# Dealing hidden features in steps of four, with 8 KB rows of w_out, in a fused attention and MLP kernel

## The chip, the core and the metric

The kernel runs on one core of one Trainium2 chip. Its time is that of one execution on the device, in microseconds. A core has five engines with an instruction stream each: TensorE (PE in the profile, its weight loads PEld), VectorE (DVE), ScalarE (ACT), GpSimd (POOL) and SyncE (SP). Transfers run on 16 DMA engines. Matmuls write to eight accumulator banks of 128 partitions and 512 four-byte words (PSUM); all else lies in the on-chip buffer (SBUF).

## The reference

There are 4 batches, 8 heads, 768 tokens and 64 features a head. Linear attention with a decay `lam` per head is computed in blocks of tokens, and its result, as rows of 512 features, goes through an MLP of 2048 hidden features with a "snake" activation.

```
intra = (q_b @ k_b.T * Dmask) @ v_b                   # inside a block; Dmask[i,j] = lam**(i-j), i >= j
inter = (q_b * lam_pow) @ kv_state                    # from the blocks before
out_b = intra + inter
kv_state = lam_block * kv_state + (k_b * rev_pow).T @ v_b

x = out as (3072 tokens, 512 features)
h = x @ w_in                                          # 512 x 2048
s = sin(alpha * h)
g = h + s * s / (alpha + 1e-9)                        # alpha: one number for each of the 2048 features
y = g @ w_out                                         # 2048 x 512
```

The order of the 2048 hidden features is free, as long as w_in's columns, alpha and w_out's rows follow the same one.

## The kernel before

Tokens are worked in six steps t of 128 tokens for all four batches, so a step has 512 columns. The MLP of a step is its group g. The hidden features are 16 blocks f of 128. Weights stand in four tiles of 512 features each: `w_in0` to `w_in3` (128 partitions by 4 pieces of x's features by 512 columns) and `w_out0` to `w_out3` (128 partitions by 4 blocks by 512). Block f takes columns `(f % 4) * 128` onward of `w_in` tile `f // 4`, one after the other; partition p of `w_out` tile i has the four rows `i * 512 + f * 128 + p`, each 2 KB in memory. All these loads turn four-byte numbers into two-byte ones and are issued by GpSimd, each into the same queue (q0); a transfer can be issued when the eighth before it has landed.

The first step is written out by hand. Its keys come in their natural form and are turned by TensorE (`turn_k0`, L383, with weight loads that take every second element); masks and the first hidden blocks run in halves of 256 columns (`hidden_half`, L458), as soon as two of the batches are done. `w_in0` is loaded in two parts of 256 columns, so that blocks 0 and 1 need the first part and blocks 2 and 3 the second. Between these matmuls stand `spin` matmuls on a constant tile. `alpha` is loaded as 16 rows of 128 and turned by one transpose (L204).

All that follows is the string `ORDER`: one word for each piece of work, in the order in which it is given to the engines. Each engine takes its own pieces strictly in that order, so a piece that waits holds up all behind it on its engine.

| word | piece | engine |
|---|---|---|
| `I`i, `W`i | load w_in tile i, w_out tile i | GpSimd queue |
| `r`t, `R`t, `n`t, `v`t | load raw keys, raw queries (four transfers each), natural keys, values (two each) of step t | GpSimd queue |
| `d`t.p | decay half the natural keys (L263) | GpSimd |
| `k`t.p, `j`t.p | turn half the keys, half the queries (L242) | VectorE |
| `F`t.p:banks | scores of two batches, into four banks (L252) | TensorE |
| `m`t.p.a | mask of bank a (L258) | VectorE |
| `K`t, `S`t.n, `B`/`C` | new state: products (L272), sum (L281, in step 0 a copy on ScalarE), cast on ScalarE or GpSimd | TensorE, VectorE |
| `O`t:banks | outputs: `carried` (64 matmuls) and `inside` (32), into four banks (L293, L302) | TensorE |
| `x`t.a | bank a of the outputs to x (L312) | VectorE |
| `h`g.f:bank | hidden block f, four matmuls (L324) | TensorE |
| `s`g.f | sine (L329) | ScalarE |
| `q`, `P`, `Q` g.f | square, on ScalarE, or on VectorE in two ways | ScalarE, VectorE |
| `t`g.f | finish: g = h + s²/alpha (L344); it frees the bank of h | VectorE |
| `u`g.m.part:bank | 128 rows of the result, with four hidden blocks (L351), needs `w_out` tile `part` | TensorE |
| `o`g.m | copy and store | ScalarE, SyncE |

Raw tiles have one buffer each, so the loads of step t+1 wait until step t's have been turned. `inside` runs over pairs of batches:

```
for a in range(NA):            # for pair 0, and then again for pair 1
    for u in range(2):
        for n in range(NQ):
            ... O[a][half[n], 2 * pr + u] += v.T @ masked scores
```

so that every one of the four banks gets its last matmul in the second pass.

Of the kernel before, what the change touches and what calls it, by code (L numbers as in the profile page):

```python
# [10 lines left out]
FP32 = mybir.dt.float32  # L11
# [5 lines left out]
s0.0 s0.1 P0.0 P0.1 I1 h0.7:6 s0.2 h0.5:5 s0.3 t0.0 q0.2 t0.1 h0.4:4 h0.6:2 I2 h0.9:7 t0.2 q0.3 t0.3 s0.4 s0.5  # L17
h0.8:0 P0.4 P0.5 s0.6 q0.6 t0.6 s0.7 s0.8 t0.4 q0.7 h0.11:1 s0.9 t0.5 h0.10:3 s0.10 P0.8 t0.8 q0.9 q0.10 t0.9
s0.11 d0.1 I3 h0.12:2 s0.12 W0 t0.7 u0.1.0:5 r1 h0.15:4 t0.10 q0.11 k1.0 q0.12 h0.13:7 s0.13 t0.12 W1 h0.14:6
t0.11 s0.14 s0.15 R1 u0.0.0:0 u0.3.0:3 q0.13 W2 k1.1 q0.14 u0.1.1 q0.15 t0.14 d0.0 K0:21 S0.1 u0.3.1 t0.13 W3  # L20
t0.15 j1.0 u0.2.0:1 S0.0 u0.2.1 j1.1 F1.0:4672 m1.0.0 m1.0.2 m1.0.3 u0.2.2 u0.3.2 u0.1.2 m1.0.1 F1.1:7246 m1.1.2
v1 u0.3.3 u0.1.3 o0.3 o0.1 m1.1.3 C0.1 u0.0.1 m1.1.1 C0.0 m1.1.0 O1:3745 x1.0 x1.2 x1.3 R2 u0.0.2 u0.2.3 o0.2
u0.0.3 x1.1 o0.0 r2 j2.0 h1.0:7 s1.0 k2.0 Q1.0 h1.1:0 h1.2:2 h1.3:4 s1.1 q1.1 t1.0 t1.1 F2.0:6351 m2.0.0 n1 n2
m2.0.1 s1.2 s1.3 k2.1 q1.2 t1.2 q1.3 h1.4:7 s1.4 h1.5:0 s1.5 q1.4 q1.5 h1.6:3 t1.3 s1.6 m2.0.2 h1.7:6 m2.0.3
t1.4 s1.7 h1.8:2 t1.5 q1.6 q1.7 h1.10:4 t1.6 s1.8 h1.9:5 s1.9 s1.10 t1.7 j2.1 h1.12:7 u1.0.0:1 q1.8 t1.8 q1.9
t1.9 q1.10 t1.10 h1.11:3 d1.1 d1.0 s1.11 K1:06 u1.0.1 h1.13:2 q1.11 t1.11 h1.14:5 u1.2.0:3 v2 S1.0 d2.1 S1.1
d2.0 K2:40 u1.2.1 s1.12 q1.12 s1.13 q1.13 h1.15:6 t1.12 t1.13 S2.0 u1.0.2 s1.14 r3 q1.14 t1.14 R3 s1.15
F2.1:4572 q1.15 S2.1 t1.15 u1.2.2 m2.1.0 B2.0 u1.1.0:0 v3 B1.0 m2.1.2 m2.1.1 B1.1 u1.0.3 u1.2.3 o1.2 B2.1 m2.1.3
O2:5672 j3.0 u1.1.1 u1.1.2 k3.0 x2.0 x2.1 o1.0 x2.3 x2.2 F3.0:4156 m3.0.0 u1.1.3 o1.1 h2.0:7 s2.0 m3.0.1 h2.1:2
k3.1 q2.0 s2.1 q2.1 j3.1 m3.0.2 h2.2:0 s2.2 n3 d3.0 u1.3.0:1 h2.3:4 u1.3.1 q2.2 t2.0 t2.1 t2.2 s2.3 d3.1  # L30
F3.1:3257 m3.1.1 m3.1.2 m3.0.3 u1.3.2 q2.3 K3:02 S3.1 h2.4:5 S3.0 m3.1.3 m3.1.0 R4 s2.4 q2.4 h2.5:6 h2.6:2 s2.5
s2.6 q2.5 t2.3 t2.5 u1.3.3 q2.6 t2.6 j4.0 r4 h2.7:0 s2.7 o1.3 h2.10:4 q2.7 t2.7 h2.8:7 s2.8 v4 O3:2613 t2.4
h2.9:0 x3.0 x3.2 h2.13:5 q2.8 s2.9 x3.3 s2.10 n4 d4.1 h2.11:2 x3.1 u2.0.0:1 q2.9 h2.12:6 t2.8 t2.9 u2.0.1 q2.10
t2.10 h3.0:3 s2.11 q2.11 t2.11 k4.0 s2.12 q2.12 t2.12 u2.0.2 s2.13 q2.13 F4.0:4207 m4.0.0 m4.0.2 t2.13 m4.0.1
B3.0 h2.14:6 s2.14 u2.3.0:4 q2.14 h2.15:0 s2.15 q2.15 u2.3.1 t2.14 k4.1 h3.2:5 m4.0.3 s3.0 q3.0 t2.15 t3.0
h3.1:6 s3.1 q3.1 s3.2 h3.3:2 r5 t3.1 u2.0.3 u2.1.0:7 q3.2 t3.2 s3.3 j4.1 h3.4:0 q3.3 t3.3 u2.1.1 d4.0 u2.3.2
o2.0 s3.4 q3.4 t3.4 u2.1.2 F4.1:6315 m4.1.3 B3.1 u2.3.3 o2.3 m4.1.1 u2.1.3 o2.1 m4.1.0 m4.1.2 u2.2.0:2 K4:04
S4.1 S4.0 O4:1365 h3.5:4 s3.5 h3.6:0 x4.0 u3.1.0:7 x4.1 h3.8:1 s3.6 x4.2 q3.5 t3.5 q3.6 k5.0 h3.7:6 v5 u2.2.1
x4.3 t3.6 s3.7 q3.7 s3.8 u3.0.0:3 u2.2.2 q3.8 h3.9:5 s3.9 q3.9 h3.10:4 s3.10 q3.10 t3.7 R5 j5.1 j5.0 t3.8 u3.0.1
h3.11:0 u2.2.3 t3.9 t3.10 s3.11 q3.11 t3.11 o2.2 u3.1.1 h3.12:1 F5.0:6042 h3.13:5 m5.0.0 u3.1.2 m5.0.3 m5.0.1  # L40
# [16 lines left out]
def kernel(  # L57
# [11 lines left out]
    nc = tc.nc  # L69
    P = nc.NUM_PARTITIONS  # L70

    B, H, S, D = q.shape
    T = 128
    NT = S // T
    NA = 4
    NQ = H // NA
    R = T // 32
    DM, DFF = moe_w_in.shape
    NDC = DM // P
    NFC = DFF // P  # L80
# [5 lines left out]
    consts = ctx.enter_context(tc.tile_pool(name="consts", bufs=1))  # L86
# [11 lines left out]
    def bank(nm, n):  # L98
        return psum.tile([P, 512], FP32, name=nm, tag=f"b{n}")

    V, G, A = nc.vector, nc.gpsimd, nc.scalar
# [5 lines left out]
    half = [slice(D * n, D * n + D) for n in range(NQ)]  # L107
# [4 lines left out]
    raw, nat = {}, {}  # L112
# [20 lines left out]
    w_in_sb = [wpool.tile([P, NDC, 512], BF16, name=f"w_in{i}") for i in range(4)]  # L133
    w_out_sb = [wpool.tile([P, 4, DM], BF16, name=f"w_out{i}") for i in range(4)]

    def load_w_in(i, parts=1, only=None):
        w = 512 // parts
        for j in range(parts) if only is None else [only]:
            for n in range(NQ):
                G.dma_start(out=w_in_sb[i][half[n], :, j * w:(j + 1) * w], in_=moe_w_in[  # L140
                    n * 256:(n + 1) * 256, i * 512 + j * w:i * 512 + (j + 1) * w].rearrange("(c p) g -> p c g", p=D))

    def load_w_out(i):
        G.dma_start(out=w_out_sb[i][:], in_=moe_w_out[i * 512:(i + 1) * 512, :].rearrange("(f p) d -> p f d", p=P))
# [5 lines left out]
    alpha_fp = consts.tile([NFC, P], FP32, name="alpha_fp")  # L150
    A.dma_start(out=alpha_fp[:], in_=moe_alpha.rearrange("(f p) -> f p", p=P))
# [17 lines left out]
    idf = consts.tile([NFC, NFC], FP32, name="idf")  # L169
    V.tensor_scalar(out=iden[:], in0=dist[:], scalar1=0.0, scalar2=None, op0=ALU.is_equal)  # L170
    V.tensor_copy(out=idf[:], in_=iden[0:NFC, 0:NFC])
# [31 lines left out]
    a_ps = bank("a_ps", 5)  # L203
    nc.tensor.transpose(out=a_ps[:, 0:NFC], in_=alpha_fp[:], identity=idf[:])  # L204
# [92 lines left out]
    def inside(t, pr):  # L297
        for a in range(NA):
            for u in range(2):
                for n in range(NQ):  # L300
                    b = 2 * pr + u
                    nc.tensor.matmul(out=att["O"][a][half[n], b, :], lhsT=nat["v", t][:, b, 4 * n + a, :],  # L302
                                     rhs=st[t, pr][:, a, u, n, :], start=False, stop=True,
                                     skip_group_check=True)

    def outputs(t, bks):
        carried(t, bks)
        inside(t, 0)
        inside(t, 1)
# [11 lines left out]
    def hidden(g, f, n):  # L321
        hps[g, f] = bank("hps", n)
        for c in range(NDC):
            nc.tensor.matmul(out=hps[g, f][:], lhsT=w_in_sb[f // 4][:, c, (f % 4) * P:(f % 4 + 1) * P],  # L324
                             rhs=xt[g][:, c, :], start=(c == 0), stop=(c == NDC - 1))
# [94 lines left out]
    A.copy(out=alpha_sb[:], in_=a_ps[:, 0:NFC])  # L420
    cut(0)
    cut(1)
    load_w_in(0, 2, 0)
    cut(2)
    cut(3)
    load_w_in(0, 2, 1)
# [26 lines left out]
    def hidden_half(f, pr, cs):  # L453
        if pr == 0 and cs[0] == 0:
            hps[0, f] = bank("hps", FIRST[f])
        cols = slice(2 * pr * T, 2 * pr * T + 2 * T)
        for c in cs:
            nc.tensor.matmul(out=hps[0, f][:, cols], lhsT=w_in_sb[0][:, c, f * P:(f + 1) * P], rhs=xt[0][:, c, cols],  # L458
                             start=(c == 0), stop=(c == NDC - 1), skip_group_check=True)
# [8 lines left out]
    hidden_half(0, 0, (0, 1))  # L468
    hidden_half(1, 0, (0, 1))
# [3 lines left out]
    hidden_half(0, 0, (2, 3))  # L473
    hidden_half(1, 0, (2, 3))
# [3 lines left out]
    for f in (2, 3):  # L478
        hidden_half(f, 0, range(NDC))
    for f in (0, 1):  # L480
        hidden_half(f, 1, (0, 1, 2))
    for f in (0, 1):
        hidden_half(f, 1, (3,))
    for f in (2, 3):
        hidden_half(f, 1, range(NDC))
# [74 lines left out]
```

## Time and profile before

| what | before |
|---|---|
| runs | 210.05, 211.65 and 210.81 us; median 210.81 |
| the profiled execution | 212.81 us; its span, from the first instruction to the last, 211.1 us |
| TensorE's granted clock | 0.998 |
| share of the span busy | TensorE 94%, VectorE 67%, ScalarE 67%, GpSimd 38% |
| hidden blocks (L324), products with w_out (L351) | 85.4 us and 85.3 us of TensorE |
| TensorE matmuls | 2038 recorded |
| transfers of GpSimd's queue | 60144 packets, 15.47 MB |
| w_out load, from issue to landing | 9.9 us in the middle |

An instruction's duration (379 ns for a matmul of 512 columns) is longer than the distance from one to the next (four take 0.86 us in the chain of waits), because they overlap. A busy TensorE is therefore told from its gaps: the bracket at the end of a timeline row says how long the engine stood idle before the row, and what it waited for.

### The profile page before, as it was taken

The numbers are of one execution on the slowest core, as the hardware profiler recorded it, in microseconds if no ns is written. First come the engines' busy times: TensorE is split into PE (matmuls) and PEld (weight loads), VectorE is DVE, ScalarE is ACT, GpSimd is POOL, SyncE is SP. The second block draws the span as 40 slices with busy tenths as digits, with TensorE's granted clock in tenths as the row PEclk, the third lists the DMA queues.
The fourth block names the chain that finished last, engine by engine and source line by source line (L and its number), as shares of the span: only waits on it lengthen the run. The fifth ranks groups of instructions, "written<-read, shape, count | busy, mean of one in ns | idle before, by whom it ended". The sixth has DMA issues, their size and how long they took to land.

```text
span 211.1 us, 4948 instructions
## 1 busy us (share of the span) xinstructions
PE 197.4 (94%) x2038; PEld 98.5 (47%) x2065; DVE 141.8 (67%) x213; ACT 142.2 (67%) x250; POOL 81.2 (38%) x103
## 2 busy tenths in 40 slices
PE   7889987999899997999999979999999999999994
PEld 4456433454444453545444634444454444444442
DVE  4485978946999859889796749577754562444400
ACT  3877996124899633787889236987749877986531
POOL 8979457648099950994059400000000000000000
PEclk9999999999999999999999999999999999999999
DMA  7999999999939999299908990000211000210032
GB/s 131 164 184 203 191 200 203 176 177 196 208 23 102 132 163 228 37 139 179 131 0 103 172 182 0 35 18 0 106 46 50 3 0 0 101 50 0 3 149 99
DMA packets 65880, 22.61 MB, mean 107 GB/s; under 512 B 46770, under 2 KB 62914, under 8 KB 65858
## 3 DMA queue, kind: packets, MB, share of 16 engines
q0 software_dynamic: 60144, 15.47, 75.5%
q1 hardware_dynamic: 5680, 6.82, 9.4%
q8 instruction: 16, 0.26, 0.5%
q14 instruction: 6, 0.05, 0.1%
q10 hardware_dynamic: 34, 0.01, 0.0%
HBM read 31.47 MB, written 6.29 MB: 179 GB/s over the span
## 4 chain that ended last, share of the span: by engine, by line
PE 59%; DMA 21%; POOL 13%; issue 4%; DVE 1%; ACT 0%; POOLq 0%; ACTq 0%
PE ops L351 26%; PE hps L324 26%; DMA nat_v<-in_v_dram 8%; DMA w_out<-in_moe_w_out_dram 6%; DMA nat_k<-in_k_dram 4%; POOL nat_k L263 3%; DMA w_in<-in_moe_w_in_dram 3%; POOL nat_v L130 2%; POOL raw_q L123 2%; POOL w_in L140 2%; PE F_ps L252 2%; PE ops L367 2%; PE O_ps L302 2%; POOL raw_k L123 1%; PE O_ps L293 1%
## 5 line engine op out<-in xcount | busy, mean ns | idle before, releaser
L351 PE MATMUL ops<-w_out,gall 128*128 128x512 bf16 x354 | 85.3, 379 | 3.5 <-DMA w_out<-in_moe_w_out_dram 2.1
L344 DVE SCALAR_TENSOR_TENSOR gall<-s,r_sb,hps 128x512 bf16<-128x512 bf16 x96 | 67.8, 737 | 30.8 <-ACT s L335 30.7
L324 PE MATMUL hps<-xt,w_in 128*128 128x512 bf16 x357 | 85.4, 379 | 0.9 <-DVE gall L344 0.4
L329 ACT ACTIVATE s_sb<-hps,alpha_sb 128x512 bf16<-128x512 f32 x96 | 63.3, 681 | 26.8 <-PE hps L324 25.7
L351 PEld LDWEIGHTS <-gall 128*128 128x128 bf16 x368 | 35.0, 98 | 44.1 <-issue 1.6
L335 ACT ACTIVATE s<-s_sb 128x512 bf16<-128x512 bf16 x90 | 54.5, 629 | 1.6
L324 PEld LDWEIGHTS <-w_in 128*128 128x128 bf16 x368 | 35.5, 98 | 42.7 <-issue 0.6
L258 DVE TENSOR_TENSOR STm<-F_ps,C 128x512 bf16<-128x512 f32 x48 | 30.3, 682 | 5.1 <-PE F_ps L252 4.9
L357 ACT COPY o_sb<-ops 128x512 f32<-128x512 f32 x23 | 13.3, 581 | 27.6 <-PE ops L351 27.5
L263 POOL TENSOR_TENSOR nat_k<-nat_k,R 128x1024 bf16<-128x1024 bf16 x10 | 18.9, 1906 | 22.3 <-DMA nat_k<-in_k_dram 22.3
L123 POOL DMA_DIRECT2D raw_q<-in_q_dram x24 | 14.0, 593 | 6.5 <-DMA w_out<-in_moe_w_out_dram 3.3
L242 DVE STREAM_TRANSPOSE turned_q<-raw_q 128x512 f32<-128x512 f32 x12 | 12.7, 1093 | 5.4 <-DMA raw_q<-in_q_dram 5.4
L312 DVE TENSOR_TENSOR xt<-O_ps,Etab 128x512 bf16<-128x512 f32 x20 | 12.4, 677 | 5.0 <-PE O_ps L302 5.0
L130 POOL DMA_DIRECT2D nat_v<-in_v_dram x12 | 14.0, 1178 | 1.1 <-DMA w_out<-in_moe_w_out_dram 1.1
L242 DVE STREAM_TRANSPOSE turned_k<-raw_k 128x512 f32<-128x512 f32 x10 | 11.0, 1095 | 3.7 <-DMA raw_k<-in_k_dram 3.7
L123 POOL DMA_DIRECT2D raw_k<-in_k_dram x20 | 11.7, 595 | 4.4 <-DMA nat_v<-in_v_dram 2.7
L130 POOL DMA_DIRECT2D nat_k<-in_k_dram x9 | 10.5, 1185 | 0.0
L252 PE MATMUL F_ps<-turned_q,turned_k 32*128 32x128 bf16 x384 | 8.3, 215 | 2.0 <-DVE xt L312 0.7
L252 PEld LDWEIGHTS <-turned_k 32*128 32x128 bf16 x384 | 6.0, 92 | 7.8 <-issue 4.4
L184 PE MATMUL spare<-fill 128*128 128x512 bf16 x16 | 7.0, 552 | 1.7 <-DVE one L165 1.5
L302 PE MATMUL O_ps<-STm,nat_v 128*64 128x128 bf16 x160 | 5.6, 221 | 1.4 <-issue 1.4
L140 POOL DMA_DIRECT2D w_in<-in_moe_w_in_dram x10 | 6.3, 644 | 1.1 <-DMA nat_v<-in_v_dram 1.1
(63 smaller groups left out, 83.9 us busy)
## 6 DMA issues: line engine op xcount, KB each, us to landing
out_dram<-o_sb SPq DMA_DIRECT2D x23, 256.0 KB, 2.9
raw_q<-in_q_dram POOLq DMA_DIRECT2D x24, 128.0 KB, 6.3
nat_v<-in_v_dram POOLq DMA_DIRECT2D x12, 256.0 KB, 7.4
raw_k<-in_k_dram POOLq DMA_DIRECT2D x20, 128.0 KB, 5.3
nat_k<-in_k_dram POOLq DMA_DIRECT2D x9, 256.0 KB, 9.7
w_out<-in_moe_w_out_dram POOLq DMA_DIRECT2D x4, 512.0 KB, 9.9
w_in<-in_moe_w_in_dram POOLq DMA_DIRECT2D x6, 256.0 KB, 6.7
raw_k<-in_k_dram SPq DMA_DIRECT2D x2, 256.0 KB, 3.5
```

Source lines behind the costliest of these rows:

```text
L123: (eng or G).dma_start(out=dst[quad[a], bs].rearrange("t b n r d -> t (b n) (r d)"), in_=src[t, a])
L130: G.dma_start(out=nat[nm, t][:, bs].rearrange("p b h e -> p (b h) e"), in_=SRC[nm][bs, :, t * T:(t + 1) * T, :].rearrange("b h p e -> p (b ...
L242: V.transpose(out=dst.rearrange("p (x t r) -> p x r t", r=R, t=32), in_=src.rearrange("p (x r d) -> p x r d", r=R, d=32))
L252: nc.tensor.matmul(out=F[a][:, u, n, :], lhsT=kt[:, :, e] if t else kt[:, e, :], rhs=KQ["q", t][quad[a], 2 * pr + u, n, :, e], start=(e == ...
L258: V.tensor_tensor(out=st[t, pr][:, a], in0=att["F", pr][a], in1=(C0 if t else C1)[:, a].unsqueeze(1).broadcast_to([P, 2, NQ, T]), op=ALU.mult)
L263: G.tensor_tensor(out=kd, in0=kd, in1=R128[:].unsqueeze(1).unsqueeze(3).broadcast_to([P, 2, H, D]), op=ALU.mult)
L324: nc.tensor.matmul(out=hps[g, f][:], lhsT=w_in_sb[f // 4][:, c, (f % 4) * P:(f % 4 + 1) * P], rhs=xt[g][:, c, :], start=(c == 0), stop=(c ...
L329: A.activation(out=s_of[g, f][:], in_=hps[g, f][:], func=ACTF.Sin, scale=alpha_sb[:, f:f + 1])
L335: A.activation(out=s2_of[g, f][:], in_=s_sb[:], func=ACTF.Square)
L344: V.scalar_tensor_tensor(out=gall[g][:, f, :], in0=s2_of.pop((g, f))[:], scalar=r_sb[:, f:f + 1], in1=hps.pop((g, f))[:], op0=ALU.mult, op ...
L351: nc.tensor.matmul(out=ops[g, m][:], lhsT=gall[g][:, f, m * P:(m + 1) * P], rhs=w_out_sb[part][:, f % 4, :], start=(f == 0), stop=(f == NF ...
L357: A.copy(out=o_sb[:], in_=ops.pop((g, m))[:])
```

## The change

1. `load_w_out`: partition p of tile i now holds the four neighbouring rows `i * 512 + 4 * p` to `+ 3`, which are one row of 8 KB in memory. Block f therefore consists of features `i * 512 + 4 * m + f % 4`.
2. `w_in_block`: the columns of block f are read from the unchanged w_in tile in steps of four. All hidden matmuls use it.
3. `alpha` is loaded as four rows of 512 and turned by four transposes, each with every fourth column.
4. `w_in0` comes in two parts by features of x (pieces 0 and 1, then 2 and 3, all 512 columns) and no longer by columns; the half blocks of step 0 are put in an order to suit it.
5. `inside` takes a bank, and all four batches in it, before the next bank.
6. `ORDER` differs from its start up to the word ahead of `d3.0`; from there on it is the same.

```diff
-    def load_w_in(i, parts=1, only=None):
-        w = 512 // parts
-        for j in range(parts) if only is None else [only]:
-            for n in range(NQ):
-                G.dma_start(out=w_in_sb[i][half[n], :, j * w:(j + 1) * w], in_=moe_w_in[
-                    n * 256:(n + 1) * 256, i * 512 + j * w:i * 512 + (j + 1) * w].rearrange("(c p) g -> p c g", p=D))
+    def load_w_in(i, cs=slice(0, NDC)):
+        for n in range(NQ):
+            G.dma_start(out=w_in_sb[i][half[n], cs], in_=moe_w_in[
+                n * 256 + D * cs.start:n * 256 + D * cs.stop, i * 512:i * 512 + 512].rearrange("(c p) g -> p c g", p=D))

     def load_w_out(i):
-        G.dma_start(out=w_out_sb[i][:], in_=moe_w_out[i * 512:(i + 1) * 512, :].rearrange("(f p) d -> p f d", p=P))
+        G.dma_start(out=w_out_sb[i][:], in_=moe_w_out[i * 512:(i + 1) * 512, :].rearrange("(p f) d -> p f d", f=4))
+
+    def w_in_block(f, c):
+        return w_in_sb[f // 4][:, c].rearrange("p (m l) -> p l m", l=4)[:, f % 4]
...
-    alpha_fp = consts.tile([NFC, P], FP32, name="alpha_fp")
-    A.dma_start(out=alpha_fp[:], in_=moe_alpha.rearrange("(f p) -> f p", p=P))
+    alpha_fp = consts.tile([4, 512], FP32, name="alpha_fp")
+    A.dma_start(out=alpha_fp[:], in_=moe_alpha.rearrange("(i x) -> i x", i=4))
...
-    nc.tensor.transpose(out=a_ps[:, 0:NFC], in_=alpha_fp[:], identity=idf[:])
+    for l in range(4):
+        nc.tensor.transpose(out=a_ps[:, 4 * l:4 * l + 4], in_=alpha_fp[:].rearrange("i (m l) -> i l m", l=4)[:, l],
+                            identity=idf[:])
...
-    def inside(t, pr):
-        for a in range(NA):
-            for u in range(2):
-                for n in range(NQ):
-                    b = 2 * pr + u
-                    nc.tensor.matmul(out=att["O"][a][half[n], b, :], lhsT=nat["v", t][:, b, 4 * n + a, :],
-                                     rhs=st[t, pr][:, a, u, n, :], start=False, stop=True,
-                                     skip_group_check=True)
+    def inside(t, a):
+        for b in range(B):
+            for n in range(NQ):
+                nc.tensor.matmul(out=att["O"][a][half[n], b, :], lhsT=nat["v", t][:, b, 4 * n + a, :],
+                                 rhs=st[t, b // 2][:, a, b % 2, n, :], start=False, stop=True, skip_group_check=True)
...
-            nc.tensor.matmul(out=hps[g, f][:], lhsT=w_in_sb[f // 4][:, c, (f % 4) * P:(f % 4 + 1) * P],
+            nc.tensor.matmul(out=hps[g, f][:], lhsT=w_in_block(f, c),
                              rhs=xt[g][:, c, :], start=(c == 0), stop=(c == NDC - 1))
...
-    load_w_in(0, 2, 0)
+    load_w_in(0, slice(0, 2))
...
-    load_w_in(0, 2, 1)
+    load_w_in(0, slice(2, NDC))
...
-    hidden_half(0, 0, (0, 1))
-    hidden_half(1, 0, (0, 1))
+    hidden_half(0, *((f, c) for f in (0, 1) for c in (0, 1)))
...
-    hidden_half(0, 0, (2, 3))
-    hidden_half(1, 0, (2, 3))
+    hidden_half(0, *((f, c) for f in (2, 3) for c in (0, 1)))
...
-    for f in (2, 3):
-        hidden_half(f, 0, range(NDC))
+    hidden_half(0, *((f, c) for f in range(4) for c in (2, 3)))
```

The words of `ORDER` that differ, sorted by engine (GpSimd's queue and TensorE from the start, with the step of the loads of t=3; what stands between is alike):

```
TensorE before  h0.7:6 h0.5:5 h0.4:4 h0.6:2 h0.9:7 h0.8:0 h0.11:1 h0.10:3 h0.12:2 u0.1.0:5 h0.15:4 h0.13:7 h0.14:6
                u0.0.0:0 u0.3.0:3 u0.1.1 K0:21 u0.3.1 u0.2.0:1 u0.2.1 F1.0:4672 u0.2.2 ... O1:3745
        after   h0.4:4 h0.6:5 h0.7:6 h0.5:2 h0.11:3 h0.9:1 h0.8:0 h0.10:4 h0.12:2 h0.14:6 u0.1.0:5 h0.13:7 u0.2.0:1
                h0.15:4 u0.0.0:0 u0.2.1 u0.3.0:3 K0:72 u0.1.1 u0.3.1 F1.0:4627 u0.3.2 ... O1:7562
        before  F2.0:6351 h1.4:7 h1.5:0 h1.6:3 h1.7:6 h1.8:2 h1.10:4 h1.9:5 h1.12:7 u1.0.0:1 h1.11:3 K1:06 u1.0.1
                h1.13:2 h1.14:5 u1.2.0:3 K2:40
        after   F2.0:6135 h1.4:7 h1.5:0 h1.6:1 h1.7:2 h1.8:6 h1.11:3 h1.9:5 h1.10:4 u1.0.0:1 h1.12:7 h1.13:2 u1.0.1
                K1:06 h1.14:5 u1.2.0:3 K2:40
VectorE before  P0.0 P0.1 t0.0 t0.1 t0.2 t0.3 P0.4 P0.5 t0.6 t0.4 t0.5 P0.8 ...      (q0.4 is ScalarE's after)
        after   P0.0 P0.1 t0.0 t0.1 t0.2 t0.3 t0.4 P0.5 t0.5 t0.6 t0.7 P0.8 ...
GpSimd  before  I1 I2 d0.1 I3 W0 r1 W1 R1 W2 d0.0 W3 v1 C0.1 C0.0 R2 r2 n1 n2 d1.1 d1.0 v2 d2.1 d2.0 r3 R3 v3 n3 d3.0
        after   I1 I2 d0.1 I3 W0 r1 W1 R1 W2 W3 d0.0 v1 C0.1 R2 C0.0 r2 n1 n2 d1.1 d1.0 v2 d2.1 d2.0 R3 r3 n3 v3 d3.0
```

## The prediction

> **What bounds the kernel now.** I read the page's busy shares and slices first, to see which engine is full and where it is not.
>
> ```profile
> PE 197.4 (94%) x2038; PEld 98.5 (47%) x2065; DVE 141.8 (67%) x213; ACT 142.2 (67%) x250; POOL 81.2 (38%) x103
> PE   7889987999899997999999979999999999999994
> DMA  7999999999939999299908990000211000210032
> q0 software_dynamic: 60144, 15.47, 75.5%
> ```
>
> TensorE is busy 94% of the span, so no change of its waits is worth more than 13.7 us. Its weak slices lie in the first 80 us, where the DMA row is full and q0, GpSimd's queue, carries nearly all. Next, the waits of TensorE (total, times, longest):
>
> ```profile
> PE ops L351 <- DMA w_out<-in_moe_w_out_dram: 2.1, 3, 1.1
> ...
> PE O_ps L302 <- issue: 1.4, 1, 1.4
> ...
> PE F_ps L252 <- DVE xt L312: 0.7, 2, 0.4
> ...
> PE F_ps L252 <- DVE turned_k L242: 0.6, 2, 0.4
> ...
> PE hps L324 <- DVE gall L344: 0.4, 1, 0.4
> ```
>
> The timelines of TensorE and VectorE place them (start, length, instruction; in brackets the idle time before and what ended it):
>
> ```profile
> 28.41 1.04 PE L351 MATMUL ops<-w_out,gall 128*128 128x512 bf16 x4 [0.75 <-DMA w_out<-in_moe_w_out_dram]
> ...
> 34.83 1.02 PE L351 MATMUL ops<-w_out,gall 128*128 128x512 bf16 x4 [1.07 <-DMA w_out<-in_moe_w_out_dram]
> ...
> 79.59 0.23 PE L252 MATMUL F_ps<-turned_q,turned_k 32*128 32x128 bf16 x2 [0.40 <-DVE turned_k L242]
> 80.11 0.21 PE L252 MATMUL F_ps<-turned_q,turned_k 32*128 32x128 bf16 x1 [0.28 <-DVE xt L312]
> 80.70 0.61 PE L252 MATMUL F_ps<-turned_q,turned_k 32*128 32x128 bf16 x29 [0.38 <-DVE xt L312]
> ```
> ```profile
> 77.52 1.10 DVE L242 STREAM_TRANSPOSE turned_q<-raw_q 128x512 f32<-128x512 f32 x1 [2.30 <-DMA raw_q<-in_q_dram]
> 78.48 1.06 DVE L242 STREAM_TRANSPOSE turned_k<-raw_k 128x512 f32<-128x512 f32 x1
> 79.39 2.46 DVE L312 TENSOR_TENSOR xt<-O_ps,Etab 128x512 bf16<-128x512 f32 x4
> ```
>
> So there are three stages. Up to 55 us TensorE waits for transfers that stand in one queue (0.75, 1.07, 0.24 for w_out; then 0.19 and 0.40 behind a turned k that waited for raw_k). From 55 to 80.7 it is full, but for 0.40+0.28+0.38 = 1.06 us ahead of F3.0: VectorE waited 2.30 us for raw_q, and k, q and then x follow in a row. From 81 us to the end it is full, but for one 1.35 us gap at 122.9 that nothing in the profile releases.
>
> **The parts of the change.**
>
> *Larger rows.* The trace's landing marks (one per DMA engine and transfer) show how far the first engine's marks lie apart while the queue is full: w_in0 pieces (256 KB read, 1 KB rows) 0.66 us; w_in1 to 3 halves (512 KB, 2 KB rows) 1.27; w_out (1 MB, 2 KB rows) 2.52. An engine has 16 rows of such a piece, so 41 ns a row of 1 KB and 79 of 2 KB: 38 ns a KB and 3 a row. Eight rows of 8 KB cost 8 x 307 = 2.46 by that line, against 2.52. With rounding I take 0.1 us a w_out, and 4 x (0.66 - 0.635) = 0.1 for w_in0. Then w_out0 lands 0.2 us earlier, w_out1 0.3, w_out3 and all behind it 0.5. Bounds: 0, if the rate is already flat, and 2.65 (the five waits up to 55 us together), if the late engine of the second rival goes. The rows' own value is nearest to the fit; of 0.5 I let 0.4 reach TensorE at 55 us, as F2.0 waits for the last raw_k (landing 52.77), VectorE's turning of it and t1.0 behind that. The Trainium skill, "DMA: Bandwidth & Descriptors", Specifications, puts the least transfer for line rate at 512 B and would make this term 0; the rows of 1 and 2 KB agree to 4%, and by the rule the time would be 209.9.
>
> GpSimd's issue of a w_out takes 0.77 us and may shorten; it gains nothing, since GpSimd waits for landings right after (3.32 us at 28.65).
>
> *w_in by steps of four.* 400 weight loads read every fourth element. The trace has contiguous loads and steps of two, none of four:
>
> ```profile
> L324 PEld LDWEIGHTS <-w_in 128*128 128x128 bf16 x368 | 35.5, 98 | 42.7 <-issue 0.6
> ...
> L191 PEld LDWEIGHTS lam_ps<-one,lam_row 1*128 1x128 f32 x8 | 0.9, 216 | 0.8 <-DVE lam_half L198 0.8
> ```
> ```profile
> 10.63 0.45 PEld L383 LDWEIGHTS <-nat_k 128*128 128x128 bf16 x8 [0.57 <-DMA nat_k<-in_k_dram]
> ```
>
> L383 takes every second element: 8 loads in 0.45 us, and the shortest is 96 ns, as long as a contiguous one. A hidden matmul streams for 216 ns (0.86 us per four in the chain), so a load of 98 is covered more than twice over. Bounds: 98, and the 219 of the four-byte loads (L200 and L204; L191 above has 216). I take 98 as the nearest row: cost 0. Without cover it is the third rival. The Trainium skill, "SBUF — State Buffer", Door 1 (the note on cachelines), wants two hits in a 16-byte line; steps of four two-byte elements give just two, so by it nothing is lost. No run here shows that yet.
>
> *First w_in in two parts by features.* The same four transfers; the first eight matmuls need part one (landing 15.36, first use 15.55), the next eight part two (16.68, used from 17.10). Order and count stay: 0. If part two were late, 0.25 us per row of four, inside the 0.75 us wait that follows.
>
> *Alpha.* Three more transposes at 4.4 us, at most 3 x 0.26 = 0.8 us on TensorE. The warming spins behind them end at 9.07 and the scores wait to 9.60 for VectorE, so 0.53 is covered; the rest would end in the wait for w_out0. 0.
>
> *Outputs bank by bank.* A bank is complete after 8 of 32 matmuls and not after 20, so x can begin 12/32 x 1.08 = 0.4 us earlier in each of five steps. VectorE waited 5.0 us there in three of them, but the next hidden block found x ready and TensorE was full: 0. Against it, the second half's mask of bank 0 is needed 12 matmuls sooner (0.4 us): the masks of step 1 end at 45.85, its outputs begin at 45.93, the other steps have more room.
>
> *The order, first group.* One square moves from VectorE (q0.4 for P0.4) to ScalarE, 0.58 us. Ten hidden blocks now stand ahead of u0.1.0 and not nine. Walked with the rows (0.86 a block, s 0.62, q 0.58, t 0.68): h0.14 waits 0.4 for bank 6, u0.1.0 runs at 28.7, u0.0.0 ends at 33.0, and u0.2.1 waits for w_out1. Both orders have 12 hidden blocks and three pieces of output done by then, so 0.75 + 1.07 become one wait of about 1.5 to 1.8: gain 0 beyond the landing. u0.3.0, K0 and the others behind u0.2.1 come to the same count before w_out2. On GpSimd W3 goes ahead of d0.0 (decay ends near 34.4, K0 at 36.5), and C0.0 behind R2 (ends near 42.9, outputs at 45.9): 0. r2's issue slips 0.6, but its third and fourth part waited for landings anyway (44.43, 46.67).
>
> *The order, t=3.* R3 is issued ahead of r3, n3 ahead of v3. Before, k landed first, but j3.0 stands ahead of k3.0 on VectorE, and both waited for raw_q (77.40). Now q lands where k did (73.90), j3.0 runs when the masks end (75.2), and only k3.0 waits. That takes 78.48 - 77.52 = 0.96 us off VectorE's row ahead of F3.0. By the old spacing the last wait of F3.0 ends 2.22 us after k3.0 starts (78.48 to 80.70): 77.40 - 0.4 + 0.1 + 2.22 = 79.3, and TensorE arrives at 79.19 - 0.4 = 78.8. v3 then lands at 86.0, and K3 runs at 88.9; d3 and R4 come 3 us sooner, where nobody waits.
>
> **Sum.** 0.96 + 0.4 = 1.36 us, span 211.1 to 209.7. The profiled execution took 212.81, 2.00 over the median of the runs, so it becomes 211.45, and the median 210.81 becomes **209.5 us**.
>
> **Rivals.**
>
> *A late engine is freed: 207.4.* The marks show one of sixteen engines behind the others: 0.3 us at the last w_in (24.47 against 24.17), 1.66 after w_out0 (28.36, 26.70), 2.75 at w_out1 (34.79, 32.04). TensorE waits for that one. The Trainium skill, "DMA: Bandwidth & Descriptors", Latency and other measured facts, names two engines as usually slower and guesses at the fetching of descriptors; w_out has a quarter as many now. For it: the jump of 1.3 lies inside w_out0. Against it: w_out1 and w_out2 added nothing, and some jumps stand beside 16 KB instruction transfers (29.46). If it goes, the waits of 2.65 and most of the 1.06 vanish, about 3.4.
>
> *The gain is not there: 210.4.* If raw_k is later in the runs than in the profile, or the new order meets waits of its own from 55 to 79 us (h1.6 at its bank 0.15, h1.10 0.1, u1.2.0 at t1.11 up to 0.5), F3.0 is no earlier and only the 0.4 stays.
>
> *Weight loads become the bound: slower.* Steps of four decide from 216 ns a load. At 219: 32 x (219 - 116) = 3.3 us in the half blocks (24 of them took 2.79 us now), of which the 1.8 us waits cover all but 1.5, and 368 x 3 = 1.1; with the forecast's gain 210.81 + 2.6 - 1.36 = 212.1. At three times 98 it would be 368 x 78 = 28.7 and more, about 240. For it: no row has this step. Against it: a step of two costs nothing.
>
> **How the numbers follow.** About 1% is what a measurement of this kernel can tell from no change. The forecast has 0.50: 0.33 within 1% (from 208.7 up), 0.17 beyond, since the late engine differs between runs. Freed engine 0.22, faster. No gain 0.10, within. Weight loads 0.18, slower. So faster 0.39, same 0.43, slower 0.18. The range reaches to the freed engine (207.4, less 0.4) below, and above past 212.1 to 213; the slow loads beyond that are left out.
>
> **What would show it.** Right: F3.0 follows one turning, not two, and waits under 0.6 us; the wait ahead of u0.2.1 is one of 1.5 to 1.8; w_out lands 2.4 to 2.5 us apart; L324's loads stay near 98 ns. Wrong: those loads above 200, w_out1 landing before 33, or new waits of TensorE after 81 us.

## The result, and the profile after

| what | before | changed |
|---|---|---|
| median of 22 runs each | 211.03 us | 209.62 us |
| ratio, with its 95% interval | 1 | 0.9947 [0.9922, 0.9972] |
| TensorE matmuls recorded | 2038 | 2041 |
| packets of GpSimd's queue | 60144 | 58096 |

The change saves 0.53% of the time (0.28% to 0.78%), about 1.1 us; the medians lie 1.41 us apart. The ratio leaves out executions that were slow as a whole, the profiled one of the changed kernel (212.41 us) among them, and the medians do not. The forecast was 209.5 us, from a sum of 1.36 us. In that profiled execution (span 210.7 us) TensorE's granted clock was 0.83 between 116 and 126 us, so its rows are compared with others only up to the gap in O4 near 119 us, and its span not at all. What the clock has to do with that gap comes with the gap below.

The page of the changed kernel: the busy shares, the slices of TensorE and of the DMA engines (tenths, 40 slices), and GpSimd's queue.

```profile
PE 198.4 (94%) x2041; PEld 105.4 (50%) x2068; DVE 141.6 (67%) x212; ACT 142.2 (67%) x251; POOL 80.5 (38%) x103
...
PE   7789998999899999999999699999999999999994
...
DMA  7999999999959999999059930100311000210032
...
q0 software_dynamic: 58096, 15.47, 74.3%
```

The picture is the same: TensorE is full but for the first 80 us and one slice near 117 to 122 us. The queue moves the same 15.47 MB with 2048 packets fewer, which is the rows of w_out. New is PEld, 98.5 us before: the weight loads take longer.

The waits of TensorE in the changed kernel (total, times, longest):

```profile
PE O_ps L304 <- issue: 2.0, 1, 2.0
...
PE ops L352 <- DMA w_out<-in_moe_w_out_dram: 0.6, 1, 0.6
...
PE hps L325 <- DVE gall L345: 0.4, 1, 0.4
PE F_ps L256 <- DVE turned_k L246: 0.3, 1, 0.3
```

The waits for w_out fell from 2.1 to 0.6, those of F (the scores' matmuls) for x are gone, and the gap in O4 (`issue`, for which the profile names nothing) is still there. Next the places: TensorE's timeline around w_out1 and around F3.0, then VectorE's ahead of F3.0.

```profile
33.51 1.89 PE L352 MATMUL ops<-w_out,gall 128*128 128x512 bf16 x8 [0.59 <-DMA w_out<-in_moe_w_out_dram]
...
76.40 1.67 PE L352 MATMUL ops<-w_out,gall 128*128 128x512 bf16 x7 [0.16 <-issue]
78.01 0.64 PE L256 MATMUL F_ps<-turned_q,turned_k 32*128 32x128 bf16 x32
78.58 1.04 PE L352 MATMUL ops<-w_out,gall 128*128 128x512 bf16 x4
```
```profile
74.02 1.09 DVE L246 STREAM_TRANSPOSE turned_q<-raw_q 128x512 f32<-128x512 f32 x1
75.45 1.14 DVE L246 STREAM_TRANSPOSE turned_k<-raw_k 128x512 f32<-128x512 f32 x1 [0.34 <-DMA raw_k<-in_k_dram]
76.41 2.49 DVE L313 TENSOR_TENSOR xt<-O_ps,Etab 128x512 bf16<-128x512 f32 x4
```

Before, 32 matmuls of F3.0 came in three pieces with 0.40, 0.28 and 0.38 us of idle time. Now they are one row of 0.64 us that starts as the products ahead of it end. VectorE turned q as soon as its masks were done, and only k waited, 0.34 us where the pair had waited 2.30.

To place a saving, three marks are read from TensorE's timeline of each kernel. "Before" and "changed" in this order: F2.0 starts at 54.06 and 52.82 us; F3.0 ends 27.25 and 25.83 us later; K4 starts 38.28 and 38.32 us after that. So of the 2.62 us by which K4 is earlier, 1.24 come ahead of F2.0, 1.42 between F2.0 and the end of F3.0, and nothing from there on. That is one execution of each; how far such marks can be trusted is what the experiments had to say.

### The profile page after: what moved, and what is told of

The parts are those of the page before. It is cut to its first block, busy times and chain, and to the rows that moved or that the text cites. A ratio compares the mean times of both kernels' runs of the same rounds, so it can differ in the third digit from the quotient of the medians.

```text
span 210.7 us, 4951 instructions
## 1 busy us (share of the span) xinstructions
PE 198.4 (94%) x2041; PEld 105.4 (50%) x2068; DVE 141.6 (67%) x212; ACT 142.2 (67%) x251; POOL 80.5 (38%) x103
## 3 DMA queue, kind: packets, MB, share of 16 engines
q0 software_dynamic: 58096, 15.47, 74.3%
## 4 chain that ended last, share of the span: by engine, by line
PE 71%; DMA 13%; POOL 10%; issue 3%; DVE 1%; ACT 0%; POOLq 0%; DVEq 0%; ACTq 0%
PE hps L325 32%; PE ops L352 31%; DMA raw_k<-in_k_dram 8%; DMA nat_v<-in_v_dram 5%; POOL w_in L139 3%; PE O_ps L304 2%; PE F_ps L256 2%; POOL nat_k L267 2%; PE ops L368 2%; POOL nat_v L130 2%; PE O_ps L297 1%; PE KV_ps L276 1%; POOL raw_q L123 1%; POOL C L228 1%; POOL nat_k L130 1%
## 5 line engine op out<-in xcount | busy, mean ns | idle before, releaser
L345 DVE SCALAR_TENSOR_TENSOR gall<-s,r_sb,hps 128x512 bf16<-128x512 bf16 x96 | 68.0, 739 | 33.6 <-ACT s L336 33.4
L325 PE MATMUL hps<-xt,w_in 128*128 128x512 bf16 x357 | 86.6, 382 | 1.1 <-DVE gall L345 0.4
L325 PEld LDWEIGHTS <-w_in 128*128 128x128 bf16 x368 | 41.2, 114 | 38.6 <-issue 1.9
L336 ACT ACTIVATE s<-s_sb 128x512 bf16<-128x512 bf16 x91 | 55.6, 638 | 1.6
L304 PE MATMUL O_ps<-STm,nat_v 128*64 128x128 bf16 x160 | 6.1, 232 | 2.0 <-issue 2.0
L186 PE MATMUL spare<-fill 128*128 128x512 bf16 x16 | 6.2, 494 | 1.7 <-DVE one L167 1.5
```

What stands on the lines that cost most here:

```text
L325: nc.tensor.matmul(out=hps[g, f][:], lhsT=w_in_block(f, c), rhs=xt[g][:, c, :], start=(c == 0), stop=(c == NDC - 1))
L336: A.activation(out=s2_of[g, f][:], in_=s_sb[:], func=ACTF.Square)
L345: V.scalar_tensor_tensor(out=gall[g][:, f, :], in0=s2_of.pop((g, f))[:], scalar=r_sb[:, f:f + 1], in1=hps.pop((g, f))[:], op0=ALU.mult, op ...
```

## The experiments

Every kernel gave one profile, and all but three were timed against the kernel before. The table collects what all of them showed, with times in microseconds. "F2.0 starts" counts from the start of the span, "F2.0 to end of F3.0" and "then to K4" are the two stretches behind it. "Gap" is the idle time inside O4. The column beside it says when the 16 KB instruction transfer next to it began, counted from the start of K4.

| kernel | ratio [95%] | F2.0 starts | F2.0 to end of F3.0 | then to K4 | gap | transfer begins |
|---|---|---|---|---|---|---|
| before | 1 | 54.06 | 27.25 | 38.28 | 1.35 | +0.74 |
| changed | 0.9947 [0.9922, 0.9972] | 52.82 | 25.83 | 38.32 | 1.96 | +1.00 |
| t3_only | 0.9977 [0.9939, 1.0014] | 52.91 | 26.20 | 38.28 | 2.97 | +2.33 |
| no_t3 | 1.0011 [0.9972, 1.0050] | 52.51 | 26.69 | 38.33 | 1.18 | +0.49 |
| rows_only | 0.9984 [0.9947, 1.0021] | 53.95 | 26.42 | 38.33 | 1.54 | +0.40 |
| no_rows | 0.9979 [0.9933, 1.0026] | 52.39 | 25.11 | 38.28 | 1.69 | +1.27 |
| pairs | 0.9968 [0.9933, 1.0003] | 52.43 | 25.88 | 38.32 | 0.92 | +0.38 |
| step2 | one run, 209.34 us | 52.60 | 25.71 | 38.28 | 0.92 | +0.33 |
| step8 | one run, 208.94 us | 51.71 | 25.82 | 38.41 | 1.00 | +0.41 |
| step16 | one run, 211.39 us | 53.58 | 25.82 | 38.41 | 1.56 | +0.52 |
| before_v5 | 1.0014 [0.9979, 1.0049] | 53.32 | 26.87 | 38.27 | 0 | -0.34 |
| v5_early | 0.9895 [0.9859, 0.9930] | 52.06 | 25.75 | 38.33 | 0 | -0.42 |
| t3_v5 | 0.9943 [0.9902, 0.9984] | 52.16 | 26.53 | 38.28 | 0.71 | -0.35 |
| v5_again | 0.9906 [0.9871, 0.9940] | 52.62 | 25.74 | 38.33 | 0.84 | -0.51 |

### The order of t=3, alone and taken back

```diff
 t3_only: the kernel before, with
-  ... s1.14 r3 q1.14 t1.14 R3 s1.15 ... B2.0 u1.1.0:0 v3 B1.0 ... s2.2 n3 d3.0
+  ... s1.14 R3 q1.14 t1.14 r3 s1.15 ... B2.0 u1.1.0:0 n3 B1.0 ... s2.2 v3 d3.0
 no_t3: the changed kernel, with
-  ... R3 q1.14 t1.14 r3 ... n3 ... v3 d3.0
+  ... r3 q1.14 t1.14 R3 ... v3 ... n3 d3.0
```

> The kernel before, with only the loads of step 3 in the new order (R3 ahead of r3, n3 ahead of v3). If most of the gain comes from one turning instead of two ahead of F3.0: 0.9 to 1.1 us faster than before (ratio near 0.995), the three waits at F3.0 (1.06 us together) gone or under 0.6, and w_out landings as before. If the gain comes from the rows: no change in time, and the waits at F3.0 only move.

> The changed kernel, with the loads of step 3 back in the old order (r3, R3, v3, n3). If the t=3 order carries most of the gain: 0.9 to 1.1 us slower than the changed kernel, so 0.3 to 0.5 us faster than before (ratio 0.998), and F3.0 waits about 1 us again. If the rows carry it: as fast as the changed kernel (ratio near 0.995).

Measured: 0.9977 with the move alone (0.49 us, where 0.9 to 1.1 were expected), 1.0011 with all the rest but not the move (0.998 was expected). Neither interval leaves out 1, so the timings alone settle nothing; the rows say more. TensorE's timeline at F3.0 in no_t3, and VectorE's ahead of it:

```profile
77.62 0.58 PE L256 MATMUL F_ps<-turned_q,turned_k 32*128 32x128 bf16 x3
78.58 0.62 PE L256 MATMUL F_ps<-turned_q,turned_k 32*128 32x128 bf16 x29 [0.38 <-DVE xt L313]
```
```profile
75.36 1.12 DVE L246 STREAM_TRANSPOSE turned_q<-raw_q 128x512 f32<-128x512 f32 x1 [1.65 <-DMA raw_q<-in_q_dram]
76.33 1.08 DVE L246 STREAM_TRANSPOSE turned_k<-raw_k 128x512 f32<-128x512 f32 x1
```

And TensorE's in t3_only:

```profile
78.31 0.80 PE L252 MATMUL F_ps<-turned_q,turned_k 32*128 32x128 bf16 x32
```

With the old order two turnings follow the landing, and F3.0 is broken again by the wait for x, although the layout is the new one. With the new order in the old layout, in t3_only, F3.0 is whole. Over all executions of the table, F2.0 to the end of F3.0 took 26.81 us on average in the four kernels with the old order (26.42 to 27.25) and 25.84 us in the ten with the new one (25.11 to 26.53). (t3_v5 is the longest of the ten: F2.0 came early there, k3.0 waited 1.37 us for raw_k, and F3.0 is in two pieces again.) The difference is 0.97 us, and the stage behind it is 38.3 us in all of them, so nothing of it is given back there.

### The layout, alone and taken back

```diff
 rows_only: the changed kernel with the ORDER of before and outputs by pairs
 no_rows:   the kernel before with the changed ORDER and outputs by banks
 step2:     the changed kernel, with rows of 4 KB and steps of two (alpha's transposes in steps of two as well)
-    ... moe_w_out[i * 512:(i + 1) * 512, :].rearrange("(p f) d -> p f d", f=4))
+    ... moe_w_out[i * 512:(i + 1) * 512, :].rearrange("(y p f) d -> p y f d", y=2, f=2))
-        return w_in_sb[f // 4][:, c].rearrange("p (m l) -> p l m", l=4)[:, f % 4]
+        return w_in_sb[f // 4][:, c].rearrange("p (y m l) -> p y l m", y=2, l=2)[:, f % 4 // 2, f % 2]
```

> The changed layout (8 KB rows of w_out, steps of four, alpha, w_in0 by features) with the old ORDER and outputs by pairs. By my sum: 0.4 us faster than before (ratio 0.998), F3.0 waits about 1 us as before, w_out transfers 2.4 to 2.5 us apart. If the larger rows free the late engine: 1.5 us or more faster, and its lag behind the fifteenth at w_out1 under 1 us. If they are worth nothing: the same as before.

> The kernel before (2 KB rows, contiguous weight loads, w_in0 by columns) with the new ORDER and outputs bank by bank. By my sum: 0.95 us faster than before (ratio 0.9955), weight loads of L324 98 ns, w_out transfers 2.52 us apart. If the rows carry the gain: the same as before or slower. If the new first group has a price of its own, one long wait for w_out1 of over 1.8 us and a time between.

> The changed kernel with the features dealt in steps of two: rows of w_out of 4 KB (two for each partition and tile), w_in's columns in steps of two, alpha to match. If a load's time goes by the 16-byte lines that it touches, with a floor (98 ns for 16 lines, 114 for 64, 144 for 128): 98 ns for 32 lines, as the turning of step 0 had. If every step beyond one costs: between 98 and 114. w_out transfers 2.45 to 2.52 us apart.

Measured: 0.9984, as expected, 0.9979, where 0.9955 was expected, and one run of 209.34. Neither ratio differs from 1 by more than its interval, and one run alone says little. The transfers themselves can be read better. The first engine's landing marks of a w_out and of the transfer ahead of it lie, for w_out0 and w_out3, 2.39 and 2.46 us apart in the changed kernel, 2.47 and 2.50 in no_t3, 2.43 and 2.47 in rows_only, all with rows of 8 KB. With rows of 2 KB they lie 2.52 and 2.58 apart before, 2.54 and 2.54 in t3_only, 2.51 and 2.57 in no_rows. Over a longer stretch the two kinds don't overlap: from the last w_in's first mark to w_out3's, with four w_out and the same eight other transfers in it, it took 15.18 to 15.39 us in the eight executions with 8 KB rows and 15.47 to 15.60 in the five with 2 KB. That is 0.31 us for four, so a w_out is about 0.08 us shorter.

What of it reaches TensorE is not shown. F2.0 starts 1.26 to 1.30 us after the last raw_k has landed in 13 of the 14 executions (1.91 in no_rows). It starts at 52.71 us on average over the eight executions with 8 KB rows, and at 52.97 over the five with 2 KB rows. But t3_only, t3_v5, before_v5 and the kernel before issue the same instructions up to F2.0, and there it starts anywhere from 52.16 to 54.06. A difference of 0.26 us between means is not one that 13 executions with such a spread can tell from nothing.

A rival stands beside the rows here: the order of the first group, which the prediction put at 0. Sorted by it, F2.0 starts at 53.28 us on average in the five executions with the old order and at 52.52 in the nine with the new one, further apart than by rows. rows_only, with the new layout and the old order, starts it at 53.95, and no_rows, the other way round, at 52.39. The ranges overlap (52.16 to 54.06 and 51.71 to 53.58), so this is not shown either, but what comes ahead of F2.0 may be due to the order and not to the rows.

The late DMA engine of the prediction's second rival does not hang on the rows. At w_out1 the last engine's mark lay 2.74 us behind the fifteenth before, and 0.44 in the changed kernel. With 2 KB rows it lay 0.35 behind in t3_only, 0.46 in no_rows and 0.56 in before_v5. So at w_out1 the engine is on time without any change of the rows. And a late one comes with 8 KB rows too, at another place: in no_t3 the last mark lies 2.57 us behind the fifteenth at one of step 2's key transfers. Why one is late in one execution and not in the next stays open.

### Outputs by pairs again

```diff
 pairs: the changed kernel, with
-        for a in range(NA):
-            inside(t, a)
+        inside(t, 0)
+        inside(t, 1)
 and `inside` itself as in the kernel before, a pair of batches over all banks
```

> The changed kernel with outputs by pairs of batches again, instead of bank by bank. By my prediction no change (ratio near 0.995): x begins about 0.4 us later in each step where VectorE waits, and TensorE has other work. If bank by bank is worth its 0.4 us a step on the path: 1 to 2 us slower than the changed kernel (ratio 1.000 to 1.004).

Measured: 0.9968, against 0.9947 with banks, well inside both intervals. VectorE's first x of O1 begins 0.89 us after `inside` does in pairs and 0.46 us after in the changed kernel: 0.43 us earlier, as the change says. F2.0 to the end of F3.0 takes 25.88 and 25.83 us. The earlier x is there and TensorE does not need it.

### Wider steps through w_in

```diff
 step8, step16: the changed kernel; hidden blocks read every 8th, every 16th column
-            nc.tensor.matmul(out=hps[g, f][:], lhsT=w_in_block(f, c),
+            nc.tensor.matmul(out=hps[g, f][:], lhsT=w_in_far(f, c),
```

> The changed kernel, but the full hidden blocks (L325 there) read their 128 columns of a w_in tile in steps of eight and not of four, over two of its pieces, so that h has other weights than the reference; the half blocks of step 0 and all else as in the change. The load took 98 ns contiguous and 114 in steps of four. If a load's time goes by the 16-byte lines that it touches (16, 64 and now 128 of them): 140 to 165 ns, still under the 216 of a matmul, and the time as the changed kernel's. If it jumps beyond two hits a line: over 216, and each of 368 matmuls slower by the excess (260 ns would make 16 us).

> As with steps of eight, but in steps of sixteen, over all four pieces of a w_in tile (h again has other weights than the reference). Lines touched stay at 128: by lines the load takes as long as in steps of eight. If the step itself counts, it is longer again, and perhaps over 216 ns, so that TensorE shows it: four hidden matmuls over 0.87 us.

The groups of weight loads (busy time, mean ns of one, idle time ahead of them), for the changed kernel, then step2, step8 and step16:

```profile
L325 PEld LDWEIGHTS <-w_in 128*128 128x128 bf16 x368 | 41.2, 114 | 38.6 <-issue 1.9 <-DVE STm L262 0.5
```
```profile
L325 PEld LDWEIGHTS <-w_in 128*128 128x128 bf16 x368 | 35.3, 98 | 42.7 <-DVE STm L262 0.5 <-issue 0.4
```
```profile
L328 PEld LDWEIGHTS <-w_in 128*128 128x128 bf16 x368 | 52.2, 144 | 28.2 <-issue 0.5 <-DVE STm L265 0.4
```
```profile
L328 PEld LDWEIGHTS <-w_in 128*128 128x128 bf16 x368 | 52.2, 145 | 28.1 <-issue 0.5 <-DVE STm L265 0.4
```

A load takes 98 ns with the columns side by side or in steps of two, 114 in steps of four, 144 in steps of eight and 145 in steps of sixteen. The last equality matters: from steps of eight on, each 16 bytes of the buffer hold one wanted element, and it gets no worse. So the times fit the number of 16-byte pieces that the 128 elements touch: 16, 32, 64, 128, 128, with no difference between 16 and 32. The Trainium skill, "SBUF — State Buffer", Door 1 (the note on cachelines), asks for two hits in such a piece for full bandwidth. Steps of four have two and still cost 16 ns, so the measurement differs from the page there; it agrees that one hit is worse. Hardly any of it reaches the matmuls: F3.0's end to K4, a stage that is full of hidden blocks, takes 38.27 or 38.28 us at 98 ns, 38.32 or 38.33 at 114 (no_t3, rows_only and the kernels by v5 among them), and 38.41 at 144 and 145: 0.05 and 0.13 us more in 38. A load stays well below the 216 ns for which a matmul streams.

### The gap in O4

The waits of the changed kernel left one thing to explain, which was in the kernel before too: TensorE stops inside O4 and nothing in the profile releases it. These are TensorE's timelines, of before and of the changed kernel:

```profile
120.91 0.64 PE L302 MATMUL O_ps<-STm,nat_v 128*64 128x128 bf16 x16
122.90 0.64 PE L302 MATMUL O_ps<-STm,nat_v 128*64 128x128 bf16 x16 [1.35 <-issue]
```
```profile
118.28 0.53 PE L304 MATMUL O_ps<-STm,nat_v 128*64 128x128 bf16 x12
120.77 1.28 PE L304 MATMUL O_ps<-STm,nat_v 128*64 128x128 bf16 x20 [1.96 <-issue]
```

In every kernel that has the gap it falls after 12 to 16 of the 32 matmuls of `inside`, and a 16 KB transfer of the instruction queue (q8 of the page) runs beside it. Q8 makes 16 such transfers, and TensorE has 4109 recorded matmuls and weight loads, 257 for each transfer. The Trainium skill, "Runtime: NRT & Kernel Launch", Instruction fetch mechanics, says that each engine gets its instructions in blocks of 16 KiB, 256 instructions, through a DMA queue of its own, and that crossing into the next block is mostly hidden. The count here agrees with the block; whether this one is hidden was to be tried. The place in the stream of instructions is the same each time. From the start of K4 to the gap the profiles record 286 to 288 matmuls and weight loads in the four kernels with the old layout that have the gap, and 280 to 282 in the eight with the new one, whose three more transposes for alpha put 6 more records ahead of K4. TensorE stops there 1.84 to 1.95 us after K4's start. At that time GpSimd's queue carries v5 and R5. The experiment moves v5, which nobody needs before step 5:

```diff
 v5_early: the changed kernel; before_v5: the kernel before; in both
-  ... s2.10 n4 d4.1 ...        k5.0 h3.7:6 v5 u2.2.1 ...
+  ... s2.10 n4 v5 d4.1 ...     k5.0 h3.7:6 u2.2.1 ...
 t3_v5: t3_only with the same move; v5_again: v5_early once more, on the chip of t3_v5
```

> The changed kernel with v5 (the values of step 5, two transfers) issued right behind n4 and no longer behind d4.0. Every profile so far has a gap of TensorE in the middle of O4 that nothing releases (1.2 to 3.0 us). If a 16 KB transfer of TensorE's own instructions stands behind v5 and R5 in the DMA engines there: the gap falls under 0.8 us and the time by 0.7 to 1.5 us against the changed kernel (ratio to before near 0.990). If the gap has to do with the instructions alone: it stays at 1.2 to 3.0 and the ratio near 0.995.

> The kernel before, with nothing but v5 issued right behind n4. With the changed kernel this took the gap in O4 away and 0.5% of the time. If the gap comes from transfers in front of TensorE's instructions, it must be as large here: gap under 0.3 us and 1.0 to 1.8 us faster than before (ratio 0.992 to 0.995). If it was a property of the new order: gap and time as before.

> The kernel before, with only two moves in its order: the t=3 loads as in the changed kernel (R3 ahead of r3, n3 ahead of v3) and v5 right behind n4. Theory that both moves act by themselves and the layout gives nothing that can be seen: about 1.0 us for t=3 and 0.9 to 1.4 us for the gap of O4, so a ratio of 0.989 to 0.991, and no wait of O4 in the profile. Theory that the gap is worth nothing outside a profiled execution (v5 moved alone gave 1.0014): 0.995 to 0.998, as for the t=3 loads alone. Theory that the layout is needed for the better result: over 0.994, and above v5_again run beside it.

> The changed kernel with v5 right behind n4, once more, beside t3_v5 on one chip. If 0.9895 was a true value: 0.986 to 0.993, and no wait of O4 in the profile. If the gap is worth nothing outside a profiled execution: the changed kernel's own 0.9947, give or take 0.003. Against t3_v5: equal within 0.003 if the 8 KB rows, the steps of four, the outputs by banks and the first group's order give nothing that can be seen; 0.004 (0.8 us) lower if they are worth what the forecast gave them (0.4 us) or more.

TensorE's timeline of v5_early has O4 in one piece. That of v5_again, the same kernel, has a gap, but a shorter one:

```profile
117.45 1.42 PE L304 MATMUL O_ps<-STm,nat_v 128*64 128x128 bf16 x32
```
```profile
118.00 0.53 PE L304 MATMUL O_ps<-STm,nat_v 128*64 128x128 bf16 x12
119.36 0.75 PE L304 MATMUL O_ps<-STm,nat_v 128*64 128x128 bf16 x20 [0.84 <-issue]
```

The DMA view for 110 to 122 us (queue, kind: packets, MB, and the times of all packets added up, as a share of the 16 engines' time), of the changed kernel and of v5_again:

```profile
q0 software_dynamic: 5765, 1.31, 121.5%
...
q8 instruction: 1, 0.02, 0.7%
```
```profile
q0 software_dynamic: 1636, 0.79, 54.7%
...
q8 instruction: 2, 0.03, 1.5%
```

Three things hold together. First, with v5's packets moved away (less than a third is left in this pair), the instruction transfer begins 0.34 to 0.51 us ahead of K4 in all four kernels with v5 early, and 0.33 to 2.33 us behind it in all ten others. Second, in the 12 executions with a gap TensorE resumes 1.17 to 1.60 us after that transfer's end, however long the transfer took (0.96 to 2.02 us). Third, the gap averages 0.39 us with v5 early (0, 0, 0.71, 0.84) against 1.51 us without (0.92 to 2.97). So the gap is the wait for a block of instructions, as far as place and times can tell, and the traffic of v5 makes it longer; that the transfer is held up in a queue behind that traffic is argued from these times and not seen by itself. Why the wait shows here and not at the other 15 transfers is argued too: it takes 2.3 to 3.2 us from the transfer's start until TensorE goes on, and from K4 to the gap TensorE runs through some 285 short instructions in 1.84 to 1.95 us.

A long gap costs more than itself. In the two executions with the longest ones, changed (1.96 us) and t3_only (2.97), the granted clock is 0.50 for 3.4 us, from 120.7 us and from 122.6 on: as the gap ends, and 0.3 us after it. Two stretches of the changed kernel, in the gap and behind it (length, busy time and number of matmuls, granted clock, DMA share, GB/s):

```profile
118.00:120.00 2.00, 0.81 (x52) 1.00 1.33 158
...
122.00:124.00 2.00, 1.78 (x5) 0.50 0.39 106
```

From the start of K4 to F5.0, without the gap itself, these two take 17.16 and 17.21 us, the twelve others, at full clock, 15.5 to 15.7: another 1.4 to 1.7 us. Two executions don't show which length of gap brings this on, nor that nothing else does.

What moving v5 is worth in time is less certain. From the changed kernel to v5_early and v5_again the ratio falls by 0.0052 and 0.0041, and from t3_only to t3_v5 by 0.0034, where 1.1 us would be 0.0053. But from before to before_v5 it rises by 0.0014, although that profile has no gap. That miss stays open; the expectations that the move alone would be seen in every kernel failed there. t3_v5 missed as well: 0.9943 and a gap of 0.71 us, where the two moves by themselves were to give 0.989 to 0.991 and no gap. v5_again came to the ratio that was expected, and its gap did not go. Its distance to v5_again, run beside it, is 0.0037 (0.78 us), near the 0.004 that was expected if the rest of the change is worth its 0.4 us or more; the two intervals overlap, so this is no proof. Both timings of the changed kernel with v5 early have medians, 209.02 and 209.22 us, below the 209.62 of the changed kernel, though from other sets of runs. The mean granted clock of each timed execution points the same way: it is 0.992 or less, as in the two profiles with a long gap, in 1 of 48 executions with v5 early and in 25 of 183 without, and 0.997 or more in all others. Where in these executions the clock was lower is not on record.

## Why the prediction was right, and where it was not

**The t=3 order, 0.96 us: right, in size and place.** F3.0 follows one turning and, in the changed kernel, does not wait at all; the list of signs had under 0.6 us. The profiles give 0.97 us. The five timed pairs that differ by this move (t3_only to before, changed to no_t3, no_rows to before, changed to rows_only, t3_v5 to before_v5; the third and fourth differ in the outputs and the first group's order too) give 0.49, 1.35, 0.44, 0.78 and 1.50 us, 0.9 on average. They share runs, and each is uncertain by some 0.8 us or more, so they support the size and don't fix it.

**The larger rows, 0.4 us: right for a transfer, not shown in the end.** The prediction's line gave 0.06 us a w_out and took 0.1 with rounding; 0.08 was measured. That 0.4 us of it reach TensorE, no run shows, and the order of the first group, put at 0, may have moved F2.0 as much. The timed pairs for the layout, with or without the rest but for the t=3 order (rows_only to before, changed to t3_only, v5_again to t3_v5, no_t3 to before) give 0.34, 0.63, 0.78 and -0.23 us, 0.4 on average, with none of them outside its noise. That the whole, about 1.1 us, came out near the sum of 1.36 is therefore in part luck: only its 0.96 us are seen in the rows.

**The waits for w_out: wrong.** One wait of 1.5 to 1.8 us was forecast ahead of u0.2.1, and it was 0.59. The step that failed was to take w_out1's landing, 34.79 us, from the profile as a property of the kernel: 2.74 us of it were one late engine of that execution. In the other 13 executions w_out1 landed between 32.1 (no_t3) and 33.6 us (step2), at 33.47 in the changed kernel. In eight of them it landed before 33, which the prediction had as a sign of being wrong. The total did not suffer, because F2.0 waits for raw_k and not for w_out. For the same reason the second rival had no case for 207.4: where the late engine was gone without the new rows (t3_only, before_v5, t3_v5), F2.0 started 1.15, 0.74 and 1.90 us earlier and not 2.65.

**The weight loads, 98 ns: the cost of next to nothing was right, the load itself was mis-sized.** They took 114, which was inside the bounds and under the cover of 216, and F3.0 to K4 grew by 0.05 us. The third rival fell with the 145 ns of steps of sixteen: no step of two-byte elements tried here comes near 216.

**Outputs by banks: right.** x begins 0.43 us earlier without effect, as forecast. The first w_in by features, alpha and the first group's order have no kernel to themselves, so nothing is shown of them alone.

**The rival without the gain, 210.4,** is not what the timing says: the whole interval lies below 0.9972, or 210.2 us against 210.81. Left out of the prediction was the gap in O4, which was read as a fixed 1.35 us. It is the most variable stretch behind 81 us, 0 to 2.97 us from execution to execution, and with the lower clock behind the long ones it moves a run by more than the whole change does.

## What to carry to other kernels

A wait in one profile is a sample. Before a forecast leans on a landing time, look at whether one DMA engine alone made it, and whether the next wait would take its place. Where two transfers feed one engine in a fixed order, issue first the one that the engine takes first: that could be seen in the rows here, where the effect of larger transfers on TensorE could not. And an idle stretch with no releaser, beside an instruction transfer and a full queue, is worth an experiment that moves traffic which isn't urgent: here it shortened the stretch in each of four profiles, and the timing was lower in three of four.

## What was not expected of the hardware

- A 128-column load of two-byte weights takes 98 ns in steps of one and two, 114 in steps of four, 144 and 145 in steps of eight and sixteen.
- TensorE stood for 0.7 to 3.0 us at one place of its instructions in 12 of 14 profiles, until 1.17 to 1.60 us after a 16 KB instruction transfer had ended. Behind the two longest stops its granted clock was 0.50 for 3.4 us.
- The same instructions reached F2.0 at 52.16 to 54.06 us in four executions, each time 1.27 to 1.29 us after the last raw_k had landed: that alone is nearly 1% of the time.
